# The second expert pair's second layer as seven block products over F in two halves, with its output stored transposed

## The chip, the cores and the metric

The kernel runs on one core of one Trainium2 chip. The metric is the device time of one execution in microseconds (us): 1131.18 us, the median of three runs (1131.17 to 1131.72). TensorE (PE in the rows) multiplies, VectorE (DVE) and ScalarE (ACT) do the elementwise work, SyncE (SP) issues nearly all DMA transfers, GpSimd (POOL) issues four.

## The reference, cut to what matters

```python
# retention over (batch 4, heads 8, seq 768, dim 64), then two dense experts on 3072 tokens x 512
x = attn_out.transpose(0, 2, 1, 3).reshape(B * S, H * D)          # 3072 x 512
x = _moe_ref(x, **moe);    # h = x @ w_in (512x2048); g = h - tanh(h);  x = g @ w_out (2048x512)
y = _moe2_ref(x, **moe2)   # h = x @ w_in;  g = where(h > 0, h, exp(min(h, 0)) - 1);  y = g @ w_out
```

Everything is float32. F below is the inner dimension of 2048; an "expert pair" is w_in with w_out. The change is in the last line, g @ w_out of the second pair.

## The kernel before, in words

**Arithmetic.** A float32 operand is split in two fp32r parts, a high part (a copy by ScalarE) and a low part (operand minus high part, by VectorE). A product of two operands takes three matmuls, high*high, high*low and low*high, all issued in `three` (L388, the matmul is L392). A matmul has a 128x128 stationary operand and 512 moving columns.

**Stages.** First comes retention, interleaved with the first expert pair over six blocks of 512 tokens; its result goes to DRAM (`x1d`). The weights of the second pair are unpacked meanwhile and stored as split operands: `w2d` for w_in (`weight_quad`, eight "quads" j of two 128-wide slices f = j and j + 8), `w3d` for w_out (`weight_split` and `weight_store`, 16 slices f). Then the second pair runs three times, for p = 0, 1, 2, on two blocks (1024 tokens) each.

**The second pair's first layer** is already done by Strassen's scheme in Winograd's form. Tokens are halved, the 512 input features are halved, and the two slices of a quad are the halves of F. `tokens` builds seven split token operands (`xh1`/`xl1` to `xh7`/`xl7`) from r11, r12, r21, r22. Each quad takes seven products of six matmuls, in three PSUM banks x, w, z, in the order 1, 2, 6, 7, 5, 4, 3; a product of a higher number in the list may add to a bank that an earlier one filled, and `snap` (ScalarE) or `plus` (VectorE) takes the bank's value in between. A quad's weights come as one load of 1792 KB (`q`).

**The second pair's second layer** is direct. For p, the 16 slices of F of the first token half (rows 11 and 12) are multiplied into four banks `acc3a`, the stationary operand being a 128-token piece of g and the moving one a w3 slice (512 KB load each, again for `acc3b`). The second token half is held in `ys` and multiplied into `acc3b` afterwards. Each slice is 4 banks x 3 matmuls. `split_g` makes g's two parts. The `acc3a` matmuls stand between the first layer's products (`filler`, `tails`), the `acc3b` ones behind them.

**What sets the order.** All operations after the start are given to a planner (`Plan`). Its list of TensorE operations is kept as written; the other engines' operations are ordered by due times, with tile slots and quotas per group (four `g` tiles, for instance) as limits. Each engine then runs its list in order and waits on semaphores.

Of the kernel before, what the change touches and what calls it, by code (L numbers as in the profile page):

```python
# [18 lines left out]
P = 128  # L19
TB = 512  # L20
# [226 lines left out]
def retention_moe_kernel(ctx: ExitStack, tc: tile.TileContext, dims, ins, out):  # L247
# [27 lines left out]
    w2d = [dram.tile([P, 14, HW], F32R, name=f"w2d{j}") for j in range(NQ)]  # L275
    w3d = [dram.tile([P, 2, TB], F32R, name=f"w3d{f}") for f in range(NF)]
# [120 lines left out]
    with tc.manual_schedule():  # L397
# [124 lines left out]
        for i in range(4, 12):  # L522
# [20 lines left out]
            {"raw": 12, "g": 4, "qk": 2, "pt": 1, "w1r": 5, "w3r": 5, "T": 1, "wop": 4, "r3": 1,  # L543
# [9 lines left out]
        dr = {id(t): Buf("D", name="d") for t in (*x1d, *w1d, *w2d, *w3d)}  # L553
# [54 lines left out]
        def weight_quad(j, rel):  # L608

            for f in (j, j + NQ):  # L610
                weight_raw((2, f), rel, "raw2")
                weight_32((2, f), rel)
            lo_, hi_ = W32.pop((2, j)), W32.pop((2, j + NQ))
            t = Buf("A", [P, 4, HW], F32, f"wt{j}", "T")

            def T(i):
                return t.ap[:, i, :]

            q = 0.34
            op("DVE", q, lambda: sub(T(0), hi_.ap[:, 0:HW], lo_.ap[:, 0:HW]), r=[lo_, hi_], w=[(t, 0)], name="T1")  # L620
            op("DVE", q, lambda: sub(T(1), hi_.ap[:, HW:], T(0)), r=[hi_, (t, 0)], w=[(t, 1)], name="T2")
            op("DVE", q, lambda: sub(T(2), hi_.ap[:, HW:], hi_.ap[:, 0:HW]), r=[hi_], w=[(t, 2)], name="T3")
            op("DVE", q, lambda: sub(T(3), lo_.ap[:, HW:], T(1)), r=[lo_, (t, 1)], w=[(t, 3)], name="T4")
# [4 lines left out]
            op("ACT", ACT5, lambda: copy(bh.ap[:, 0:2, :], lo_.ap.rearrange("p (a n) -> p a n", a=2)), r=[lo_], w=[(bh, 0)])  # L628
            op("ACT", 0.32, lambda: copy(bh.ap[:, 2, :], hi_.ap[:, HW:]), r=[hi_], w=[(bh, 1)])
            op("ACT", 0.95, lambda: copy(th.ap, t.ap), r=[t], w=[th])  # L630
            op("DVE", DVE5, lambda: sub(bl.ap[:, 0:2, :], lo_.ap.rearrange("p (a n) -> p a n", a=2), bh.ap[:, 0:2, :].bitcast(F32)),
               r=[lo_, (bh, 0)], w=[(bl, 0)])
            op("DVE", q, lambda: sub(bl.ap[:, 2, :], hi_.ap[:, HW:], bh.ap[:, 2, :].bitcast(F32)), r=[hi_, (bh, 1)], w=[(bl, 1)])
            op("DVE", 1.14, lambda: sub(tl.ap, t.ap, th.ap.bitcast(F32)), r=[t, th], w=[tl])
            d, k = w2d[j], dbuf(w2d[j])
            for i, (b, n) in enumerate(((bh, 3), (th, 4), (bl, 3), (tl, 4))):
                at = (0, 3, 7, 10)[i]
                dma(lambda b=b, at=at, n=n: nc.sync.dma_start(out=d[:, at:at + n, :].bitcast(F32), in_=b.ap.bitcast(F32)),
                    n * 1024, r=[b], w=[(k, i)], due=60.0)
# [114 lines left out]
        def split_g(y, name, key=None, view=None, rel=0):  # L754
            g = Buf("A", [P, 2, TB], F32R, f"g{name}", "g")
            yv = (lambda: y.ap) if view is None else (lambda: y.ap[:, view, :])
            op("ACT", ACT5, lambda: copy(g.ap[:, 0, :], yv()), r=[(y, key)], w=[(g, 0)], rel=rel, name=f"ghi{name}")
# [34 lines left out]


# [28 lines left out]
        w2_from = 2 * NF  # L822
        pend = []
        acc = None
        quads = list(range(NQ))
        w3s = list(range(NF))
# [14 lines left out]
        for b, f, lo, hi in order0:  # L841
            if b == NB - 1 and f == 0:
                block5 = now_pe()
# [16 lines left out]
            if n >= w2_from and n % 6 == 1 and quads:  # L860
                weight_quad(quads.pop(0), now_pe())
            n += 1
        assert not quads and not w3s

        XH, XL = {}, {}

        def tokens(p, rel):


            R = {}
            for i in (1, 2):
                for j in (1, 2):
                    t = R[i, j] = Buf("A", [P, 2, TB], F32, f"r{i}{j}_{p}", "r")
                    for c in range(2):
                        src = x1d[2 * p + c]
                        dma(lambda t=t, i=i, j=j, c=c, src=src: nc.sync.dma_start(
                            out=t.ap[:, :, c * HW:(c + 1) * HW],
                            in_=src[:, 2 * (j - 1):2 * j, (i - 1) * HW:i * HW]),  # L880
                            2048, r=[dbuf(src)], w=[(t, c)], rel=rel, name=f"r{i}{j}_{p}")

            def split(i, t):
                h = XH[i] = Buf("A", [P, 2, TB], F32R, f"xh{i}_{p}")
                l = XL[i] = Buf("A", [P, 2, TB], F32R, f"xl{i}_{p}")
# [15 lines left out]
            split(3, a21)  # L901

        def product(i, q, xs, dst, first, last):
            h, l = xs[i]
            k = PLACE[i]

            def fn():
# [169 lines left out]
```

## Time and profile before

| | |
|---|---|
| three runs | 1131.17, 1131.18, 1131.72 us |
| the profiled execution | 1131.98 us, of which the profile's span is 1130.1 us |
| TensorE | 5889 matmuls, busy 1109.5 us (98%) |
| weight loads | 903.7 us (80%) |
| VectorE, ScalarE | 781.4 us (69%), 664.7 us (59%) |
| DMA | 239.82 MB, mean 212 GB/s |
| chain that ended last | TensorE 96%, DMA 3%, VectorE 1% |

The page's span runs from the first to the last instruction. A matmul's record (some 390 ns) is longer than the step from one matmul to the next, since records overlap; the chain cuts the overlap away, so its pieces add up to time. In the same way records on VectorE and ScalarE overlap by some 0.1 us, and the step between two starts is what one instruction costs.

### The profile page before, as it was taken

The numbers are of one execution on the slowest core, as the hardware profiler recorded it, in microseconds if no ns is written. First come the engines' busy times: TensorE is split into PE (matmuls) and PEld (weight loads), VectorE is DVE, ScalarE is ACT, GpSimd is POOL, SyncE is SP. The second block draws the span as 40 slices with busy tenths as digits, with TensorE's granted clock in tenths as the row PEclk, the third lists the DMA queues.
The fourth block names the chain that finished last, engine by engine and source line by source line (L and its number), as shares of the span: only waits on it lengthen the run. The fifth ranks groups of instructions, "written<-read, shape, count | busy, mean of one in ns | idle before, by whom it ended". The sixth has DMA issues, their size and how long they took to land.

```text
span 1130.1 us, 15594 instructions
## 1 busy us (share of the span) xinstructions
PE 1109.5 (98%) x5889; PEld 903.7 (80%) x5889; DVE 781.4 (69%) x1274; ACT 664.7 (59%) x1194; POOL 3.8 (0%) x8
## 2 busy tenths in 40 slices
PE   7699999999999999999999999999999999999998
PEld 5588888888888888878888888888888888888887
DVE  5798899667888899788867765565465573455650
ACT  2556785455566656666756766563566662655650
POOL 0000000000000000000000000000000000000000
PEclk9799999999999999999999999999999999999999
DMA  8734375426758866677580564658455656544560
GB/s 312 279 121 164 128 252 190 129 76 225 264 195 309 297 247 255 248 281 284 218 319 1 198 233 179 237 170 352 140 205 205 237 213 267 192 176 186 209 260 38
DMA packets 67497, 239.82 MB, mean 212 GB/s; under 512 B 7264, under 2 KB 13408, under 8 KB 64352
## 3 DMA queue, kind: packets, MB, share of 16 engines
q1 hardware_dynamic: 66272, 235.96, 56.2%
q0 software_dynamic: 576, 2.10, 1.1%
q8 instruction: 46, 0.75, 0.3%
q10 hardware_dynamic: 576, 0.79, 0.2%
q14 instruction: 27, 0.22, 0.1%
HBM read 192.68 MB, written 46.14 MB: 211 GB/s over the span
## 4 chain that ended last, share of the span: by engine, by line
PE 96%; DMA 3%; DVE 1%; ACT 0%; issue 0%; SPq 0%
PE acc L392 24%; PE h L392 22%; PE x L392 12%; PE acc3a L392 12%; PE acc3b L392 12%; PE z L392 6%; PE w L392 3%; PE sc L332 2%; PE oe L362 1%; PE oe L356 1%; DMA kn<-qkv 1%; PE oo L362 1%; PE oo L370 1%; DMA stage<-qkv 1%; DMA dtab<-dtab 1%; DMA raw<-w 1%
## 5 line engine op out<-in xcount | busy, mean ns | idle before, releaser
L392 PE MATMUL acc<-g,w 128*128 128x512 f32 x1152 | 281.9, 393 | 0.0
L392 PE MATMUL h<-x,w 128*128 128x512 f32 x1152 | 278.8, 391 | 0.0
L392 PEld LDWEIGHTS h<-x,w 128*128 128x128 f32 x1152 | 217.3, 189 | 45.6 <-issue 0.2
L392 PEld LDWEIGHTS acc<-g,w 128*128 128x128 f32 x1152 | 213.3, 188 | 47.2 <-issue 0.5
L288 ACT ACTIVATE g<-y 128x512 fp32r<-128x512 f32 x144 | 90.8, 631 | 123.8 <-DVE y L731 92.5
L392 PE MATMUL acc3a<-w,g 128*128 128x512 f32 x576 | 137.1, 389 | 0.0
L392 PE MATMUL x<-xh,q 128*128 128x512 f32 x384 | 134.8, 391 | 0.0
L291 DVE TENSOR_TENSOR g<-y,g 128x512 fp32r<-128x512 f32 x144 | 99.5, 691 | 46.9 <-ACT g L288 43.5
L392 PE MATMUL acc3b<-w,gb 128*128 128x512 f32 x576 | 131.7, 389 | 0.0
L392 PEld LDWEIGHTS acc3a<-w,g 128*128 128x128 f32 x576 | 108.1, 188 | 22.7
L392 PEld LDWEIGHTS acc3b<-w,gb 128*128 128x128 f32 x576 | 108.1, 188 | 22.5
L749 DVE SCALAR_TENSOR_TENSOR y<-y,t 128x512 f32<-128x512 f32 x48 | 33.2, 692 | 124.6 <-ACT t L744 124.6
L720 ACT ACTIVATE u<-h 128x512 f32<-128x512 f32 x96 | 56.9, 593 | 79.2 <-PE h L392 79.1
L726 DVE SCALAR_TENSOR_TENSOR y<-y,u 128x512 f32<-128x512 f32 x96 | 66.1, 689 | 41.4 <-ACT y L720 41.4
L392 PEld LDWEIGHTS x<-xh,q 128*128 128x128 f32 x384 | 72.0, 188 | 17.2 <-DVE z L294 1.0
L392 PE MATMUL x<-xl,q 128*128 128x512 f32 x192 | 74.9, 390 | 0.0
L731 DVE COPY_PREDICATED y<-m,h 128x512 f32<-128x512 uint16 x96 | 70.6, 735 | 4.1 <-ACT m L720 0.9
L720 ACT ACTIVATE m<-u,xs_b 128x512 bf16<-128x512 f32 x96 | 69.5, 724 | 0.0
L720 ACT ACTIVATE y<-u,qa_b 128x512 f32<-128x512 f32 x96 | 69.3, 722 | 0.0
L392 PE MATMUL z<-xh,q 128*128 128x512 f32 x192 | 68.0, 395 | 0.0
L728 DVE SCALAR_TENSOR_TENSOR y<-y,h 128x512 f32<-128x512 f32 x96 | 65.6, 684 | 2.7 <-ACT m L720 0.5
L291 DVE TENSOR_TENSOR h<-h,t 128x512 f32<-128x512 f32 x96 | 66.5, 693 | 0.0
(92 smaller groups left out, 1317.1 us busy)
## 6 DMA issues: line engine op xcount, KB each, us to landing
w<-w3d SPq DMA_DIRECT2D x96, 512.0 KB, 8.7
q<-w2d SPq DMA_DIRECT2D x24, 1792.0 KB, 7.3
raw<-w SPq DMA_DIRECT2D x64, 512.0 KB, 7.1
w<-w1d SPq DMA_DIRECT2D x64, 512.0 KB, 6.4
qk<-qkv SPq DMA_DIRECT2D x20, 512.0 KB, 5.8
w1d<-w SPq DMA_DIRECT2D x16, 512.0 KB, 2.9
w3d<-w SPq DMA_DIRECT2D x16, 512.0 KB, 3.0
v<-qkv SPq DMA_DIRECT2D x24, 256.0 KB, 6.0
```

The lines of the kernel that those rows point to most:

```text
L288: nc.scalar.activation(out=out_, in_=in_, func=AF.Copy)
L291: nc.vector.tensor_tensor(out=out_, in0=a, in1=b, op=ALU.subtract)
L332: nc.tensor.matmul(out=sc[j][:, p, :], lhsT=qk[r, 1, p * P:(p + 1) * P], rhs=qk[r, 0, p * P:(p + 1) * P], start=True, stop=True,)
L356: nc.tensor.matmul(out=outs[p][half(p, j)], lhsT=stc[r, p, :], rhs=qk[r, 0, p * P:(p + 1) * P], start=(p < 2), stop=False, skip_group_chec ...
L362: nc.tensor.matmul(out=outs[p][half(p, j)], lhsT=v[:, h * D:(h + 1) * D], rhs=pt[:, j, p, :], start=False, stop=True, skip_group_check=True,)
L370: nc.tensor.matmul(out=ds[r, p, :], lhsT=kn[:, h * D:(h + 1) * D], rhs=v[:, h * D:(h + 1) * D], start=True, stop=True, skip_group_check=True,)
L392: nc.tensor.matmul(out=out_, lhsT=lhs(a), rhs=rhs(b), skip_group_check=True, start=(first and at == 0 and i == 0), stop=(last and at == n ...
L720: op("ACT", dur, lambda: nc.scalar.activation(out=o.ap, in_=i.ap, func=func, **kw), r=r, w=w, name=f"{func}{name}")
L726: op("DVE", DVE5, lambda: nc.vector.scalar_tensor_tensor(out=y.ap, in0=y.ap, scalar=QB, in1=u.ap, op0=ALU.add, op1=ALU.mult), r=[u], w=[y])
L728: op("DVE", DVE5, lambda: nc.vector.scalar_tensor_tensor(out=y.ap, in0=y.ap, scalar=C2, in1=h.ap, op0=ALU.mult, op1=ALU.mult), r=[h], w=[y ...
L731: op("DVE", 0.65, lambda: nc.vector.copy_predicated(out=y.ap, mask=m.ap.bitcast(U16), data=h.ap), r=[m, h], w=[y], due=9.0)
L749: op("DVE", DVE5, lambda: nc.vector.scalar_tensor_tensor(out=yv(), in0=yv(), scalar=1.0, in1=t.ap, op0=ALU.add, op1=ALU.mult), r=[t], w=[k])
```

## The change

The second layer of the second pair becomes Strassen's seven products as well. Its blocks are: the two token halves (rows), F in two halves (the inner dimension: slices j and j + 8), and the 512 output features in two halves (columns).

- `weight_quad(m, j)` now makes the seven block operands for w_out too (m = 3), and stores them in one DRAM tensor `w3d`, ordered by product. The operands' low parts stand beside the high ones, also in `w2d`. The 16 calls of it are at `quad_at` and, for the last two, in the first layer of p = 0; the 16 separate splits and stores of w_out are gone.
- The first layer keeps its products but orders them 1, 7, (3 of the quad before), 6, 2, 4, 5, and loads a quad's weights in four pieces. All four results of a quad are kept in `y` (two tiles of two).
- `second_layer` forms the sums S3, S1, S2, S4 of the activations per j on VectorE, splits seven operands of eight j each, and multiplies them in the order 1, 7, 6, 5, 4, 2, 3 into the bank pairs x, z, x, x, z, w, x. The weights are now stationary and the activations move, so the result is features by tokens; each product's weights are one 2048 KB load in one of two `X` slots. Results are stored as they stand, and the host reorders the output array at the end.
- Matmuls of the second layer: before 3 x 16 slices x 2 token halves x 4 banks x 3 = 1152; now 3 x 7 products x 8 j x 2 banks x 3 = 1008.

```diff
-    w2d = [dram.tile([P, 14, HW], F32R, name=f"w2d{j}") for j in range(NQ)]
-    w3d = [dram.tile([P, 2, TB], F32R, name=f"w3d{f}") for f in range(NF)]
+    w2d = [dram.tile([P, 7, 2, HW], F32R, name=f"w2d{j}") for j in range(NQ)]
+    w3d = dram.tile([P, 7, NQ, 2, HW], F32R, name="w3d")
...
+            for i, b in enumerate(((w1, L), b21, (w2, H))):
+                op("ACT", 0.32, lambda i=i, b=b: copy(bh.ap[:, i, :], at(b)), r=[b[0]], w=[(bh, i)])
+                op("DVE", q, lambda i=i, b=b: sub(bl.ap[:, i, :], at(b), bh.ap[:, i, :].bitcast(F32)),
+                   r=[b[0], (bh, i)], w=[(bl, i)])
...
+        quad_at = [2 * NF + 3 * NF * i // 12 for i in range(12)] + [5 * NF, 5 * NF + 3]
+        quads = [(m, j) for m in (2, 3) for j in range(NQ)]
...
-            if n >= w2_from and n % 3 == 0 and w3s:
-                for _ in range(1):
-                    f3 = w3s.pop(0)
-                    weight_raw((3, f3), now_pe(), "raw2")
-                    weight_32((3, f3))
-                    weight_split((3, f3), "wop")
-                    weight_store((3, f3), w3d[f3])
...
+            product(1, x, True)
+            s1 = snap(x, f"s1_{nm}")
+            yield
+            product(7, z, True)
+            z7 = snap(z, f"z7_{nm}")
+            yield
+            yield
+            product(6, x, False)
+            u2 = snap(x, f"u2_{nm}")
+            product(2, w, True)
+            activate(plus(w, s1, f"c11_{nm}"), 11)
+            product(4, z, False)
+            activate(plus(z, u2, f"c21_{nm}"), 21)
+            product(5, x, False)
+            activate(plus(x, z7, f"c22_{nm}", 2.0), 22)
+            yield
+            product(3, x, False)
+            activate(x, 12)
...
+        def second_layer(p, prev):
...
+            def product(i, operands, dst, first, by_e=False):
+                t = Buf("X", [P, NQ, 2, HW], F32R, f"w3_{p}_{i}")
+                k = PLACE[i]
+                dma(lambda: nc.sync.dma_start(out=t.ap.bitcast(F32), in_=w3d[:, k].bitcast(F32)),
+                    16 * 1024, r=[dbuf(w3d)], w=[t], name=f"w3_{p}_{i}")
...
+                    if (j, e) == (2, 0) and i == 1:
+                        next(prev)
...
+                        three(dst[e].ap, lambda a: t.ap[:, j, a, e * P:(e + 1) * P],
+                              lambda b: g[j].ap[:, b, :], first, True, NQ, j)
...
+            product(1, operand(11), x, True)
+            s1 = [snap(x[e], f"os1_{p}_{e}") for e in range(2)]
+            product(7, [s3(j) for j in range(NQ)], z, True)
+            z7 = [snap(z[e], f"oz7_{p}_{e}") for e in range(2)]
+            product(6, operand(11), x, False)
+            u2 = [snap(x[e], f"ou2_{p}_{e}") for e in range(2)]
+            product(5, operand(21), x, False)
+            for e in range(2):
+                store(plus(x[e], z7[e], f"oc22_{p}_{e}", 2.0), 1, 1, e)
+            product(4, operand(22), z, False)
...
+            if not last:
+                tokens(p + 1)
+            product(2, operand(12), w, True)
...
+            product(3, [s4(j) for j in range(NQ)], x, False, by_e=last)
...
-                def tail(g, f, first, last, acc_a=acc_a):
-                    weight_load(3, f, w3d[f], "w3r")
-                    second(3, W[3, f], g, acc_a, first, last)
...
-    out = nc.dram_tensor("out", (B * S, DM), F32, kind="ExternalOutput").ap()
+    out = nc.dram_tensor("out", (NCH // 2, 2, KC, P, TB), F32, kind="ExternalOutput").ap()
```

**Place 1, TensorE, first layer of p = 1, quad 1.** A tile `x1_1` is bank x of p = 1, quad 1 (its last number is only a label), `xh7_1` the high part of token operand 7. Before:

```order
L392 MATMUL z1_1_7567<-xh7_1_7205,q1_1_7360 128x512
L392 MATMUL z1_1_7567<-xl7_1_7211,q1_1_7360 128x512
L392 MATMUL z1_1_7567<-xh7_1_7205,q1_1_7360 128x512 x2
L392 MATMUL z1_1_7567<-xl7_1_7211,q1_1_7360 128x512
L392 MATMUL z1_1_7567<-xh7_1_7205,q1_1_7360 128x512
L392 MATMUL x1_1_7525<-xh5_1_7252,q1_1_7360 128x512
L392 MATMUL x1_1_7525<-xl5_1_7264,q1_1_7360 128x512
L392 MATMUL x1_1_7525<-xh5_1_7252,q1_1_7360 128x512 x2
L392 MATMUL x1_1_7525<-xl5_1_7264,q1_1_7360 128x512
L392 MATMUL x1_1_7525<-xh5_1_7252,q1_1_7360 128x512
L392 MATMUL z1_1_7567<-xh4_1_7241,q1_1_7360 128x512
L392 MATMUL z1_1_7567<-xl4_1_7254,q1_1_7360 128x512
```

Now, from the end of product 7 on:

```order
L392 MATMUL z1_1_7711<-xh7_1_7481,q1_1_1_7524 128x512
L392 MATMUL x1_0_7624<-xh3_1_7649,q1_0_3_7540 128x512
L392 MATMUL x1_0_7624<-xl3_1_7663,q1_0_3_7540 128x512
L392 MATMUL x1_0_7624<-xh3_1_7649,q1_0_3_7540 128x512 x2
L392 MATMUL x1_0_7624<-xl3_1_7663,q1_0_3_7540 128x512
L392 MATMUL x1_0_7624<-xh3_1_7649,q1_0_3_7540 128x512
L392 MATMUL x1_1_7696<-xh6_1_7597,q1_1_2_7557 128x512
L392 MATMUL x1_1_7696<-xl6_1_7610,q1_1_2_7557 128x512
L392 MATMUL x1_1_7696<-xh6_1_7597,q1_1_2_7557 128x512 x2
L392 MATMUL x1_1_7696<-xl6_1_7610,q1_1_2_7557 128x512
L392 MATMUL x1_1_7696<-xh6_1_7597,q1_1_2_7557 128x512
L392 MATMUL w1_1_7749<-xh2_1_7554,q1_1_2_7557 128x512
```

Product 4 came back to bank z after one product on another bank (5). Now three lie between (3 of quad 0, then 6 and 2, of which the last row is the start), or two at a pass's first quad. On bank x, one product lay between 1 and 6 and between 6 and 5, and now two, or one between 1 and 6 at a pass's first quad.

**Place 2, TensorE, second layer.** Before (p = 0), the second token half: banks `acc3b0_0` to `_3`, stationary a piece of the activations `gb`, moving a weight slice.

```order
L392 MATMUL acc3b0_0_7142<-w3_0_6965,gb0_0_7067 128x512 x3
L392 MATMUL acc3b0_1_7149<-w3_0_6965,gb0_0_7067 128x512 x3
L392 MATMUL acc3b0_2_7156<-w3_0_6965,gb0_0_7067 128x512 x3
L392 MATMUL acc3b0_3_7161<-w3_0_6965,gb0_0_7067 128x512 x3
L392 MATMUL acc3b0_0_7142<-w3_8_7062,gb0_8_7093 128x512 x3
L392 MATMUL acc3b0_1_7149<-w3_8_7062,gb0_8_7093 128x512 x3
L392 MATMUL acc3b0_2_7156<-w3_8_7062,gb0_8_7093 128x512 x3
L392 MATMUL acc3b0_3_7161<-w3_8_7062,gb0_8_7093 128x512 x3
```

Now (p = 1), the end of product 6 and the start of product 5 in the bank pair `xo1_0`, `xo1_1`, with the split operands `g1_6_j` and `g1_5_j`:

```order
L392 MATMUL xo1_0_8349<-g1_6_5_8577,w3_1_6_8466 128x512 x3
L392 MATMUL xo1_1_8356<-g1_6_5_8577,w3_1_6_8466 128x512 x3
L392 MATMUL xo1_0_8349<-g1_6_6_8588,w3_1_6_8466 128x512 x3
L392 MATMUL xo1_1_8356<-g1_6_6_8588,w3_1_6_8466 128x512 x3
L392 MATMUL xo1_0_8349<-g1_6_7_8598,w3_1_6_8466 128x512 x3
L392 MATMUL xo1_1_8356<-g1_6_7_8598,w3_1_6_8466 128x512 x3
L392 MATMUL xo1_0_8349<-g1_5_0_8608,w3_1_5_8555 128x512 x3
L392 MATMUL xo1_1_8356<-g1_5_0_8608,w3_1_5_8555 128x512 x3
```

Four banks per slice of F became two per j and product; products 6 and 5 follow each other on the same two banks, with `snap` to read each bank in between.

**Place 3, VectorE, second layer of p = 1.** Before, during `acc3b`: the low parts `gb1_f` of the held activations, and the next pass's token operands (`xl`, `s3`, `r21`).

```order
L291 TENSOR_TENSOR gb1_9_8462<-ys1_1_7667,gb1_9_8462 128x512
L291 TENSOR_TENSOR xl1_2_8489<-r11_2_8440,xh1_2_8477 128x1024
L291 TENSOR_TENSOR gb1_2_8484<-ys1_2_7788,gb1_2_8484 128x512
L291 TENSOR_TENSOR s3_2_8501<-r11_2_8440,r21_2_8443 128x1024
L291 TENSOR_TENSOR gb1_10_8506<-ys1_2_7788,gb1_10_8506 128x512
L291 TENSOR_TENSOR xl7_2_8520<-s3_2_8501,xh7_2_8514 128x1024
L291 TENSOR_TENSOR gb1_3_8530<-ys1_3_7909,gb1_3_8530 128x512
L294 TENSOR_TENSOR r21_2_8443<-r21_2_8443,r22_2_8448 128x1024
```

Now, during products 7 and 6: `g1_6_j` are low parts for product 6, the rows on `y1_j_0` and `y1_j_1` are the sums S2 and S1 and the last quad's activations.

```order
L291 TENSOR_TENSOR g1_6_2_8541<-y1_2_0_7875,g1_6_2_8541 128x512
L294 TENSOR_TENSOR y1_7_1_8360<-y1_7_1_8360 128x512
L291 TENSOR_TENSOR y1_5_0_8156<-y1_5_1_8186,y1_5_0_8156 128x512
L291 TENSOR_TENSOR g1_6_3_8561<-y1_3_0_7967,g1_6_3_8561 128x512
L754 SCALAR_TENSOR_TENSOR y1_7_0_8344<-y1_7_0_8344,t12_1_7_8423 128x512
L291 TENSOR_TENSOR y1_6_0_8250<-y1_6_1_8267,y1_6_0_8250 128x512
L756 TENSOR_TENSOR y1_7_0_8344<-x1_7_8255,y1_7_0_8344 128x512
L291 TENSOR_TENSOR g1_6_4_8567<-y1_4_0_8059,g1_6_4_8567 128x512
L291 TENSOR_TENSOR y1_7_0_8344<-y1_7_1_8360,y1_7_0_8344 128x512
L291 TENSOR_TENSOR g1_6_5_8577<-y1_5_0_8156,g1_6_5_8577 128x512
L291 TENSOR_TENSOR g1_6_6_8588<-y1_6_0_8250,g1_6_6_8588 128x512
L291 TENSOR_TENSOR g1_6_7_8598<-y1_7_0_8344,g1_6_7_8598 128x512
```

Before, each slice needed one row here; now an operand of product 6 needs its S1, its S2 and its low part, and the last quad's activations stand among them.

## Rows read from the trace of the kernel before

**Rows 1.** The page, its head and parts 1 and 2.

```profile
span 1130.1 us, 15594 instructions
...
PE 1109.5 (98%) x5889; PEld 903.7 (80%) x5889; DVE 781.4 (69%) x1274; ACT 664.7 (59%) x1194; POOL 3.8 (0%) x8
...
PEclk9799999999999999999999999999999999999999
```

**Rows 2.** Page part 5: line, engine, operation, count, busy us, mean ns.

```profile
L392 PE MATMUL acc3a<-w,g 128*128 128x512 f32 x576 | 137.1, 389 | 0.0
...
L392 PE MATMUL acc3b<-w,gb 128*128 128x512 f32 x576 | 131.7, 389 | 0.0
L392 PEld LDWEIGHTS acc3a<-w,g 128*128 128x128 f32 x576 | 108.1, 188 | 22.7
```

**Rows 3.** The chain that ended last, whole span: start us, us, what.

```profile
87.56 2.72 PE h L392 x12
...
754.09 38.08 PE acc3b L392 x168
...
918.40 38.08 PE acc3b L392 x168
...
1082.69 43.53 PE acc3b L392 x192
```

**Rows 4.** The same chain, asked for 628 to 754 us.

```profile
628.14 1.36 PE x L392 x6
...
662.14 1.37 PE z L392 x6
663.51 1.38 PE x L392 x6
664.89 1.43 PE z L392 x6
```

**Rows 5.** Waits of the weight-load queue, 628 to 1131 us: total, times, longest.

```profile
PEld z L392 <- ACT z L288: 3.5, 18, 0.2
```

**Rows 6.** Stretches: PE, PEld, DVE, ACT, POOL busy (x), PEclk, DMA share, GB/s.

```profile
60.00:170.00 110.00, 110.00 (x583) 90.37 (x582) 99.91 (x176) 81.28 (x149) 0.00 (x0) 1.00 0.45 168
...
766.00:772.00 6.00, 6.00 (x28) 4.99 (x27) 6.00 (x7) 2.93 (x4) 0.00 (x0) 1.00 1.01 426
```

**Rows 7.** Timeline of VectorE, 647 to 667 us: start us, us, instruction.

```profile
650.62 0.68 DVE L749 SCALAR_TENSOR_TENSOR ys<-ys,t 128x512 f32<-128x512 f32 x1
651.22 0.68 DVE L749 SCALAR_TENSOR_TENSOR y<-y,t 128x512 f32<-128x512 f32 x1
```

**Rows 8.** Timeline of ScalarE, 632 to 652 us.

```profile
633.62 0.60 ACT L288 ACTIVATE z<-z 128x512 f32<-128x512 f32 x1 [0.24 <-PE z L392]
...
649.83 0.62 ACT L744 ACTIVATE y<-u 128x512 f32<-128x512 f32 x1
650.35 0.62 ACT L744 ACTIVATE t<-u 128x512 f32<-128x512 f32 x1
```

**Rows 9.** Timeline of TensorE, 620 to 640 us.

```profile
633.19 0.39 PE L392 MATMUL z<-xh,q 128*128 128x512 f32 x1
```

**Rows 10.** Page part 6: transfers, count, KB each, median us to landing.

```profile
w<-w3d SPq DMA_DIRECT2D x96, 512.0 KB, 8.7
q<-w2d SPq DMA_DIRECT2D x24, 1792.0 KB, 7.3
```

**Rows 11.** Instructions and transfers on the tile q.

```profile
DMA to landing us min/median/max: 6.9/7.3/12.5
```

**Rows 12.** Timeline of all engines, 1116 to 1131 us.

```profile
1124.20 2.64 ACT L288 ACTIVATE o3b<-acc3b 128x512 f32<-128x512 f32 x4 [34.11 <-PE acc3b L392]
1124.83 2.37 SPq L788 DMA_DIRECT2D out<-o3b  x4
```

**Rows 13.** Groups of VectorE by form.

```profile
L291 DVE TENSOR_TENSOR wtl<-wt,wth 128x1024 fp32r<-128x1024 f32 x8 | 9.7, 1216 | 0.0
...
L291 DVE TENSOR_TENSOR wbl<-w,wbh 128x256 fp32r<-128x256 f32 x8 | 3.4, 420 | 0.0
```

More of the change, by code (lines that the diff above doesn't have):

```diff
@@ L903, in product @@
[L903 to L907, printed above, removed]
-                for c in range(2):
-                    three(dst.ap, lambda a: q.ap[:, 7 * a + k, c * P:(c + 1) * P],
-                          lambda b: (h, l)[b].ap[:, c, :], first, last, 2, c)
-            op("PE", 6 * MM, fn, r=[q, h, l], w=[dst], lat=0.2, name=f"p{i}")
+            if n == 5 * NF + 6:
+                tokens(0)
+            if n in quad_at:
+                weight_quad(*quads.pop(0), now_pe())
@@ L934, in retention_moe_kernel, with plus, bank, quad @@
-        tails = []
-        def filler(k=1):
-            for _ in range(k):
-                if tails:
-                    tails.pop(0)()
-        tokens(0, block5)
+        def plus(src, t, name, due=4.0):
+            op("DVE", DVE5, lambda: add(t.ap, src.ap, t.ap), r=[src], w=[t], due=due, name=name)
+            return t
+        def bank(name):
+            return Buf("P", [P, TB], F32, name)
+        def quad(p, j, xs):
+            nm = f"{p}_{j}"
+            q = {}
+            for ab in ((1, 7), (2, 6), (5, 4), (3,)):
+                n = len(ab)
+                t = Buf("A" if n == 2 else "B", [P, n, 2, HW], F32R, f"q{nm}_{ab[0]}", "w2r" if n == 2 else None)
+                a = PLACE[ab[0]]
+                step = PLACE[ab[-1]] - a or 1
+                dma(lambda t=t, a=a, n=n, step=step: nc.sync.dma_start(
+                    out=t.ap.bitcast(F32), in_=w2d[j][:, a:a + step * (n - 1) + 1:step].bitcast(F32)),
+                    n * 2048, r=[dbuf(w2d[j])], w=[t], name=f"quad{nm}")
+                for i, k in enumerate(ab):
+                    q[k] = t, i
+            x, w, z = bank(f"x{nm}"), bank(f"w{nm}"), bank(f"z{nm}")
+            def product(i, dst, first):
+                h, l = xs[i]
+                t, k = q[i]
+                def fn():
+                    for c in range(2):
+                        three(dst.ap, lambda a: t.ap[:, k, a, c * P:(c + 1) * P],
+                              lambda b: (h, l)[b].ap[:, c, :], first, True, 2, c)
+                op("PE", 6 * MM, fn, r=[t, h, l], w=[dst], lat=0.2, name=f"p{i}_{nm}")
+            y = Y[p, j] = {}
+            for k, pair in enumerate(((11, 12), (21, 22))):
+                t = Buf("A", [P, 2, TB], F32, f"y{nm}_{k}")
+                for i, kk in enumerate(pair):
+                    y[kk] = t, i
+            def activate(c, k):
+                t, i = y[k]
+                elu(c, f"{k}_{nm}", t, i, i)
+            product(1, x, True)
[16 more added lines that the diff above has]
+            activate(x, 12)
+            yield
@@ L942, in retention_moe_kernel @@
+        Y = {}
         for p in range(NB // 2):
             xs = {i: (XH[i], XL[i]) for i in XH}
[L944 to L986 removed]
@@ L987, in retention_moe_kernel @@
-            while tails:
-                filler()
-            evict(acc_a, out_place(p, 0), f"3a{p}")
-            if p + 1 < NB // 2:
-                tokens(p + 1, now_pe())
-            acc_b = new_acc(f"3b{p}")
-            for j in range(NQ):
-                for k in range(2):
-                    f = j + k * NQ
-                    def unit(j=j, k=k, f=f, rel=max(0, now_pe() - 10), stored=stored, acc_b=acc_b, p=p):
-                        g = split_g(stored[j], f"b{p}_{f}", k, k, rel=rel)
-                        weight_load(3, f, w3d[f], "w3r")
-                        second(3, W[3, f], g, acc_b, f == 0, f == NF - 1)
-                        if f == NF - 1:
-                            evict(acc_b, out_place(p, 1), f"3b{p}", step=1 if p == NB // 2 - 1 else 2)
-                    if p + 1 < NB // 2 and j == NQ - 1:
-                        tails.append(unit)
-                    else:
-                        unit()
+            for k, prev in enumerate(quads_in_turn(p, xs)):
+                if pend:
+                    seconds(len(pend) - 1)
+                if quads and k % 4 == 1:
+                    weight_quad(*quads.pop(0), now_pe())
@@ L1009, in retention_moe_kernel @@
+            assert not quads
+            second_layer(p, prev)
         for o, t in plan.run():
```

217 lines of the change are left out of this document (106 added, 111 removed).

## The prediction

> **What bounds the kernel now.** I read the page's head first: TensorE is busy 98% of the span at a granted clock of nine tenths or more in every slice but the start [rows 1]. Busy time overstates a matmul, so I went on to the chain of waits, whose pieces add up to time: 168 matmuls in a row take 38.08 us [rows 3], so one step is 0.2267 us, where its record is 389 ns [rows 2]. Twelve take 2.72 us in the first expert pair too [rows 3]. Then I looked for stretches where TensorE is not at that step. From the end of the start at 60 us its row shows no idle time, even where VectorE is at 99.91 of 110 us [rows 6]. The second pair is not quite full: from 754.09 to 918.40 us [rows 3] stand 720 matmuls (336 of the first layer, 384 of the second), 163.20 us by the step, in 164.31 us. The rest, 1.11 us, is in small pieces: products of six take 1.38 and 1.43 us beside 1.36 [rows 4], because bank z is wanted again before ScalarE has read it, 18 times in the weight-load queue's waits [rows 5]. So the kernel is a row of matmuls, and a matmul less is worth a step as long as operands, weights and banks come in time.
>
> **The sum, part by part.** Durations are of the profiled execution, 1131.98 us (span 1130.1); the median of the runs is 0.80 below it.
>
> 1. Matmuls. 1152 of the second layer become 1008; the first layer's 1008 stay. 144 x 0.2267 = 32.64 us, all on the path, since TensorE is the chain.
>
> A page of the Trainium skill would size this otherwise. "Perfetto Trace Analysis", section "Identifying the Most-Contended Engine", takes the busy time of weight loads as TensorE's measure; by it 144 loads of 188 ns [rows 2] would be worth 27.1 us. Here the step in an undisturbed stretch is 0.2267 us, so I keep 32.64.
>
> 2. The first layer's order. Bank z gets three other products between 7 and 4 where it had one, bank x two where it had one. The small stalls go: 1.11 us in the second pass, 1.09 in the third (918.40 to 1082.69, 164.29 us), and in the first 628.14 [rows 4] to 754.09, 125.95 us for 552 matmuls, 125.12 by the step, 0.83. Sum 3.0 us; between 0 (another wait takes their place) and 3.0, and I take all of it, since every gap but one per pass at least doubles.
>
> 3. Products 6 and 5 of the second layer follow each other on one bank pair. From the start of the last matmul on a bank to its next use are four steps, 0.91 us. A snap of a full bank stands in the rows: last matmul on z starts at 633.19 [rows 9], ScalarE reads from 633.62 for 0.60 us [rows 8], so 1.03 us at least, 0.12 late. From above: in the stalled case of [rows 4] z was 7 steps away and still 0.07 late, 1.66 us, which would be 0.75 late. Near the lower end ScalarE is free, since there is little but splits to do; I take 0.3, three times, 0.9 us (0.4 to 2.3). Behind it the whole of product 5 is queued.
>
> 4. VectorE. Its rows in products 1, 7 and 6 are the tight place. From the last read of the last quad's bank x to the low part of product 6's last operand stand 48 rows; back to back they step by 0.60 us [rows 7], 29 us, while TensorE has 12 + 6 + 36 + 48 + 48 = 150 matmuls, 34.0 us, and needs that operand six matmuls before their end, 32.6. Going through the rows with the four `g` tiles, each free only when TensorE has used it, and ScalarE's copies at 0.52 us [rows 8], I find the operand always earlier than wanted, by 1.5 to 2.5 us in product 7 and least, 0.4 us, at the fifth operand of product 6 (the last row but four of place 3), where the last quad's activations stand in front. The same count over products 2 and 3, where the next pass's seven token operands come in, gives at least 0.5. So I take 0.5 us in all; at worst, with each row at its record of 0.69 [rows 7], 43 rows up to that place are 3.9 us longer, 3.5 late a pass, 10.5 us.
>
> 5. Weights of w_out. 16 plain splits become eight quads. Of VectorE's work each quad loses two low parts of 0.69 and adds four sums and three low parts of 256 columns, 0.42 each, and a large low part of 1.22 [rows 13]: 2.8 us more, 22 us in all, and each w_in quad 0.15 (three small low parts for one of 0.69 and a small one), together 23 us; ScalarE, with one copy per low part, gets less. The cover is the first pair's matmul stream: per 16 steps of it there were 2.7 quads and 5.3 splits, and are 4 quads, about the same load, for longer, up into the first pass. TensorE waited for nothing with VectorE at 91% [rows 6], so nothing; if the cover were gone, 23 us.
>
> 6. Weight loads of the second layer, 2048 KB each. Product i's slot is free when product i - 2 is done, so the load has one product, 48 x 0.2267 = 10.88 us, to land, five times a pass; the first two of a pass have free slots. The nearest row is `q` with 1792 KB, 7.3 us in the median [rows 10, 11], by size 8.3: 2.5 us to spare. The slice loads of 512 KB (8.7 us, [rows 10]) wait in a queue of their own kind. The crowded place is product 4: the load for product 2, two stores, six token loads and a piece of the next quad, 4.7 MB, are issued ahead of the load for product 3. At the 426 GB/s that the queues moved [rows 6], 4.7 + 2.1 MB take 16.0 us of the 21.76 in two products. So nothing.
>
> The Trainium skill's "DMA: Bandwidth & Descriptors", section "Specifications", gives a lower limit from DRAM, some 358 GB/s per core. By it those 6.8 MB take 19.0 us, an estimate, the spare time halves to 2.8 us, and C below would be likelier by some 0.05. The 426 GB/s of [rows 6] lies above the limit, so C stays as it is.
>
> 7. End. The last bank is read and stored by the same steps as now, ScalarE then SP [rows 12]; four reads in 2.64 us become one, but the last of the four ends 0.6 us behind the last matmul in both. Nothing, at best 0.5 us less.
>
> Sum: 1131.98 - 32.64 - 3.0 + 0.9 + 0.5 = 1097.7 us in the profiled execution's terms, 1097.0 in the median's. Own range: 1095.0 (no new stall, shorter end) to 1101 (old stalls stay, 0.75 at each bank reuse).
>
> **Rivals.**
>
> A. VectorE becomes the bound in products 7 and 6. For it: 48 rows in 32.6 us leave it 10% and it waits for ScalarE and for `g` tiles in turn, with a smallest lead of 0.4 us in a strict order. Against: the step of 0.60 is measured back to back, and the stretch from 60 to 170 us ran with VectorE at 91% and no wait of TensorE [rows 6]. By item 4's bound 10.5 us: 1107.
>
> B. Slower than before: the weight loads of item 6 come late at each product's start. Its price is 15 loads x the lateness; it cancels the 34 us from 2.3 us late on, that is from 13.2 us for a load. For it: the slowest `q` took 12.5 us [rows 11], 14.3 by size, 3.4 late: 15 x 3.4 = 51, 1148 us. Against: that one stood behind a queue of other loads; in products 7, 6 and 5 nothing else is loaded.
>
> C. Some loads late only: the two in the crowded place and a few more, 2 to 5 us each with stores and token loads ahead, up to 20 us: 1103 to 1117. For and against as in B.
>
> **How the numbers follow.** Forecast 0.80, A 0.11, C 0.06, B 0.03. Predicted is the forecast's 1097.0. The range goes from its low end to 1104, which takes in the smaller half of A and the beginning of C and leaves out below two in ten. This kernel's runs lie within 0.05% of each other, and 0.2% (2.3 us) is about what can be told from no change. All but B are faster by more: 0.96; B is slower, 0.03; 0.01 for a mixture that ends where it began.
>
> **What would show it.** Right: `acc3a` and `acc3b` gone, 4320 matmuls of this kind in place of 4464, products of the second layer at 10.88 us each in the chain, all of 1.36 us in the first layer, and a pass (672 matmuls) at 152.3 us plus some 0.5. Item 3: a wait of product 5's first matmuls on ScalarE, three or six times. A: TensorE waits for a `g` low part on VectorE in product 7 or 6, in all three passes alike. B and C: TensorE waits on a DMA into `w` at the start of a product. Item 5: the first 628 us of the chain longer than now. The prediction is wrong if a pass takes more than 154 us, or if the first pair's end moves.

## The result, and the profile after

| | before | after |
|---|---|---|
| median of the runs on one chip | 1131.45 us (1131.17 to 1132.22, four runs) | 1100.88 us (1100.19 to 1101.49, four runs) |
| the profiled execution, its span | 1131.98 us, 1130.1 us | 1101.44 us, 1099.6 us |
| first expert pair, up to the first matmul of the second | 628.14 us [rows 4] | 632.38 us |
| second pair's matmuls, to the end of the last | 498.08 us [rows 3, 4] | 463.45 us |

The ratio is 0.9729, 95% interval 0.9712 to 0.9745. The forecast was 1097.0 us, range 1095.0 to 1104.0. The second pair gave 34.6 us, which is what the first three items of the sum ask for (32.64 + 3.0 - 0.9 = 34.7). The first pair, which the forecast left where it was, took back 4.2.

The head of the page after is to be set against [rows 1], and its last line against [rows 10]:

```profile
span 1099.6 us, 15843 instructions
...
PE 1075.6 (98%) x5745; PEld 877.7 (80%) x5745; DVE 905.5 (82%) x1516; ACT 709.6 (65%) x1290; POOL 3.9 (0%) x8
...
w<-w3d SPq DMA_DIRECT2D x21, 2048.0 KB, 8.1
```

144 matmuls are gone, VectorE has 124 us more to do, and the new loads of 2 MB take 8.1 us in the median (8.3 were estimated from `q`).

The chain of the kernel after, whole span (start us, us, what), is to be set against [rows 3]:

```profile
735.74 10.88 PE xo L392 x48
746.62 11.22 PE xo L392 x48
...
899.29 11.22 PE xo L392 x48
...
1051.96 11.22 PE xo L392 x48
...
1084.94 10.89 PE xo L392 x48
```

A product of 48 matmuls is 10.88 us, 48 steps of 0.2267, except product 5 in each pass, which is 0.34 longer. The second pass, from 790.48 to 943.15 us, is 152.67: 672 steps, 152.33, and that 0.34. Nothing else in the second pair is off the step, so what is missing lies before 632 us.

TensorE's waits in the kernel after, from 100 us on (the first line is of the matmuls, the others of the weight-load queue; total us, times, longest). Before, the same question from 100 to 640 us has no line for the matmuls:

```profile
PE sc L332 <- DMA qk<-qkv: 3.0, 3, 1.2
...
PEld acc L392 <- DVE g L291: 1.0, 2, 0.6
PEld xo L392 <- ACT ou L288: 1.9, 6, 0.4
```

The last is product 5's (six waits, two banks in three passes). The first two are in the first pair. To see where the time goes, I put the starts of the same first-layer products side by side. Before, chain in three stretches:

```profile
402.78 2.72 PE h L392 x12
...
453.59 2.72 PE h L392 x12
...
590.06 2.72 PE h L392 x12
...
600.94 2.72 PE h L392 x12
```

and after:

```profile
404.09 2.72 PE h L392 x12
...
457.09 2.72 PE h L392 x12
...
593.56 2.73 PE h L392 x12
...
605.18 2.72 PE h L392 x12
```

The delay is 1.31 us at the first, 3.50 at the second and third, 4.24 at the last. By the first matmul of every first-layer step (96 of them, counted from 0), the kernel after is 0.3 us late from the start (runs differ by that much there anyway, see the end). From step 4 on the two traces run in parallel but for five jumps: 1.01 at step 58, 0.95 at 62, 1.24 at 66, and 0.31 and 0.43 at 90 and 91. So 3.2 us belong to the waits for `qk` and 0.74 to those for `g`.

The chain of the kernel after, asked for 380 to 412 us, shows one `qk` wait from its root:

```profile
391.13 1.24 DVE wtl L291
...
392.38 0.36 SPq L642
...
392.84 7.11 DMA qk<-qkv
...
399.99 1.16 PE sc L332 x16
```

and SP's timeline there shows the queue:

```profile
391.12 0.37 SPq L642 DMA_DIRECT2D w2d<-wth  x1
392.38 0.36 SPq L642 DMA_DIRECT2D w2d<-wtl  x1
392.84 0.52 SPq L379 DMA_DIRECT2D qk<-qkv  x1
```

The load of `qk` needs nothing that VectorE makes. It stands behind the quad's last store, and that store waits for `wtl`. SP runs its list in order, so the load is issued when VectorE is done, and TensorE meets it 7.1 us later. Before, the same load was issued at 381.66 us and landed 8.9 us before its use. The cause of the meeting is in `quad_at`: twelve quads now start every four steps, and retention loads are issued every four steps too, so all of the last eleven loads stand one row behind a quad's store. Eight of them land 0.4 to 3.3 us ahead of use, three do not. The place in the list alone is not the harm: before, five of the same eleven stood right behind a quad's store too. But all eleven were issued 10.2 to 17.9 us ahead of their use, and now it is 6.4 to 9.7.

### The profile page after: what moved, and what is told of

It reads as the page before. It is cut to its first block, busy times and chain, and to the rows that moved or that the text cites. A ratio compares the mean times of both kernels' runs of the same rounds, so it can differ in the third digit from the quotient of the medians.

```text
span 1099.6 us, 15843 instructions
## 1 busy us (share of the span) xinstructions
PE 1075.6 (98%) x5745; PEld 877.7 (80%) x5745; DVE 905.5 (82%) x1516; ACT 709.6 (65%) x1290; POOL 3.9 (0%) x8
## 4 chain that ended last, share of the span: by engine, by line
PE 82%; DMA 7%; DVE 7%; ACT 2%; issue 1%; SPq 1%; DVEq 0%
PE acc L392 19%; PE h L392 17%; PE xo L392 12%; PE x L392 12%; PE z L392 6%; PE zo L392 6%; PE wo L392 3%; PE w L392 3%; DMA kn<-qkv 3%; DMA qk<-qkv 2%; PE sc L332 2%; DMA raw<-w 1%; PE oe L362 1%; DVE pt L297 1%; DVE y L733 1%
## 5 line engine op out<-in xcount | busy, mean ns | idle before, releaser
L288 ACT ACTIVATE g<-y 128x512 fp32r<-128x512 f32 x240 | 141.4, 624 | 148.6 <-DVE y L736 122.8
L291 DVE TENSOR_TENSOR g<-y,g 128x512 fp32r<-128x512 f32 x240 | 160.0, 687 | 41.4 <-ACT g L288 40.4
L392 PE MATMUL xo<-g,w 128*128 128x512 f32 x576 | 133.5, 390 | 0.0
L392 PE MATMUL x<-xh,q 128*128 128x512 f32 x384 | 127.1, 389 | 0.0
L392 PEld LDWEIGHTS xo<-g,w 128*128 128x128 f32 x576 | 107.7, 188 | 23.9 <-ACT ou L288 1.9
L754 DVE SCALAR_TENSOR_TENSOR y<-y,t 128x512 f32<-128x512 f32 x96 | 65.6, 685 | 14.7 <-ACT t L749 14.7
L392 PE MATMUL zo<-g,w 128*128 128x512 f32 x288 | 66.3, 389 | 0.0
L392 PEld LDWEIGHTS zo<-g,w 128*128 128x128 f32 x288 | 54.1, 188 | 11.2
```

What stands on the lines that cost most here:

```text
L288: nc.scalar.activation(out=out_, in_=in_, func=AF.Copy)
L291: nc.vector.tensor_tensor(out=out_, in0=a, in1=b, op=ALU.subtract)
L392: nc.tensor.matmul(out=out_, lhsT=lhs(a), rhs=rhs(b), skip_group_check=True, start=(first and at == 0 and i == 0), stop=(last and at == n ...
L754: op("DVE", DVE5, lambda: nc.vector.scalar_tensor_tensor(out=yv(), in0=yv(), scalar=1.0, in1=t.ap, op0=ALU.add, op1=ALU.mult), r=[t], w=[k])
```

## The experiments

"The changed kernel" is the one above. Each run was timed beside the kernel before, whose median was 1131.45 us beside the changed kernel, 1132.34 beside the first four runs and 1131.9 beside the others. So a run is set against the changed kernel by how far each is below the kernel before; for the changed kernel that is 30.6 us. The interval of a ratio spans 2 to 4 us, so a difference of one or two is read from the traces.

**Quads two steps later.**

```diff
-        quad_at = [2 * NF + 3 * NF * i // 12 for i in range(12)] + [5 * NF, 5 * NF + 3]
+        quad_at = [2 * NF + 2 + 3 * NF * i // 12 for i in range(12)] + [5 * NF, 5 * NF + 3]
```

> The first twelve weight quads start two first-layer steps later (steps 34, 38, ..., 78 in place of 32, 36, ..., 76); nothing is added or left out. Theory (order in SP's queue): in the changed kernel the retention loads of qk wait in SP's queue behind a quad's last store, which waits for VectorE's wtl; three of them land late and TensorE waits 1.01, 0.95 and 1.24 us at first-layer steps 58, 62 and 66. With the quads shifted the stores stand 4 to 7 rows ahead of the loads, so these 3.2 us go: steps 58 to 80 start 0.3 us or less off those of the kernel before, and the time is about 1097.7 us against 1100.9. The 0.74 us at steps 90 and 91 (VectorE late with g, beside the token sums) stays or grows a little, since quads 12 to 14 now stand closer together (78, 80, 83). Rival (VectorE is simply too full, 23 us more of work whose place does not matter): the 3.2 us stay, perhaps at other steps, and the time is 1100 to 1102 us.

Measured 1098.62 us (1098.02 to 1098.90), ratio 0.9703 (0.9687 to 0.9719). SP's timeline now has the load a few rows behind the store (start to start 3.2 us) and not held by it:

```profile
374.84 0.36 SPq L642 DMA_DIRECT2D w2d<-wtl  x1
...
377.62 0.40 SPq L606 DMA_DIRECT2D w<-w1d  x1
378.06 0.62 SPq L379 DMA_DIRECT2D qk<-qkv  x1
```

No wait for `qk` is left, and against the kernel before, the first-layer steps 4 and 80 are shifted by the same amount (both 1.0 us earlier). The waits for `g` grew from 0.74 to 1.4 us, as expected with quads at 78, 80 and 83. The theory holds, the rival fails.

**The quads' stores on another queue.** The quads stay where they are; `nc.sync.dma_start` becomes `nc.gpsimd.dma_start` for their four stores.

> The four stores of each weight quad are issued on GpSimd's DMA queue in place of SP's; the quads stay at their steps and VectorE's and ScalarE's work at its place. Theory (order in SP's queue): a retention load has no store ahead of it that waits for VectorE, so the three waits for qk (3.2 us in all) go though VectorE does the same work at the same time: about 1097.7 us. Rival (VectorE too full): VectorE's part is unchanged, so 1100 to 1102 us. A third outcome would be a cost of GpSimd's own issue (64 stores more on it); the trace of the changed kernel has only a few issues there, so this is not bounded by it: were VectorE's operations to become longer beside them, the time would be over 1102 us.

Measured 1098.46 us (1097.88 to 1098.73), ratio 0.9700 (0.9686 to 0.9715). No wait for `qk` is left; the one for `g` stays, 0.73 us. Stretch 250 to 550 us (PE, PEld, DVE, ACT, POOL busy (x), PEclk, DMA share, GB/s) of this kernel,

```profile
250.00:550.00 300.00, 300.00 (x1835) 243.77 (x1834) 258.27 (x464) 183.86 (x344) 38.43 (x50) 1.00 0.70 244
```

of the changed kernel,

```profile
250.00:550.00 300.00, 297.00 (x1820) 241.14 (x1819) 255.54 (x461) 181.83 (x341) 1.82 (x2) 1.00 0.70 242
```

and of the kernel before:

```profile
250.00:550.00 300.00, 300.00 (x1834) 243.63 (x1833) 254.70 (x447) 186.71 (x340) 1.66 (x2) 1.00 0.71 254
```

VectorE is as busy in all three, 255 to 258 us, and only the changed kernel's TensorE loses 3.00 us. So the loss is not VectorE's load: it is who waits behind VectorE. The two runs are 33.7 and 33.9 us below the kernel before, 3.1 and 3.3 more than the changed kernel. In the traces 3.2 us of waits for `qk` went (in the first, less 0.7 of longer waits for `g`).

**Product 4 between 6 and 5 in the second layer** (the lines of products 5 and 4 exchanged).

> In the second layer product 4 stands between products 6 and 5 (1, 7, 6, 4, 5, 2, 3 in place of 1, 7, 6, 5, 4, 2, 3). Theory: in the changed kernel product 5 takes 11.22 us and every other one 10.88, because its first matmuls wait until ScalarE has read bank x after product 6; with product 4 between, each of the three passes is 0.34 us shorter, 152.33 us for 672 matmuls, and the time 1.0 us lower, 1099.9 us. The first pair's waits (3.9 us) stay. Rival (0.34 us is what a product costs that follows an eviction of any bank, or the wait moves to product 4 or 3): a pass stays 152.67 us and the time 1100.9 us.

Measured 1101.06 us (1098.67 to 1101.90), ratio 0.9720 (0.9706 to 0.9735): 31.3 us below the kernel before, 0.7 more than the changed kernel, which is too little to tell from none. The chain shows that what the edit was for did happen:

```profile
889.58 10.88 PE xo L392 x48
900.46 10.88 PE zo L392 x48
911.34 10.88 PE xo L392 x48
```

All products take 10.88 us, a pass 152.32. In this execution the waits for `qk` took 4.4 us in place of 3.2 (there is a fourth, at step 50), which hides 1.0 us of gain. The term is confirmed from the trace, not from the time.

**The first layer's old order** (1, 2, 3 of the quad before, 6, 7, 5, 4).

> The first layer's products of a quarter go back to the order before (1, 2, 6, 7, 5, 4; product 3 of the quarter before after product 2), the rest as in the changed kernel. Theory: item 2 of the prediction holds, 3.0 us come from the order: z is read by ScalarE after product 7 and product 4 writes it one product later, so the stalls of the kernel before on banks z and x (7 or 8 quarters in each of three passes) come back, a pass takes about 153.7 us in place of 152.67, and the time is about 1103.9 us. Rival (the stalls came from ScalarE and VectorE being busy with the old second layer's operands, not from the order): a pass stays within 0.2 us of 152.67 and the time is 1100.9 us.

Measured 1103.44 us (1102.34 to 1104.59), ratio 0.9745 (0.9730 to 0.9760). The time is near the theory's 1103.9, but it is 28.9 us below the kernel before, so some 1.7 are lost and not 3.0, and not by the theory's cause. No wait on z or x is there. The first pass is 0.07 us longer and the third 0.10; the second is 1.28 longer, nearly all of it at the start of product 3, whose weights come late:

```profile
PE xo L392 <- DMA w<-w3d: 0.9, 1, 0.9
```

So the order did not bring the stalls back. The new copies had another edit on them that I had not priced, a due time of 2 us, by which the planner may put a copy ahead of activations. Two runs ask for it.

**No due time for the first layer's copies** (`s1`, `z7`, `u2` made with `due=None`), new order:

> The first layer keeps the changed kernel's product order, but its three copies of a bank by ScalarE (s1, z7, u2) lose their due time of 2 us and are ordered like the activations, as in the kernel before. The run with the old order and this due time showed no stalls on z and x, so the due time alone removes them. Theory 1 (order or due time, either one is enough): no stalls here, a pass 152.67 us, the time 1100.9 us. Theory 2 (the due time alone does it, the order nothing): the copies come behind activations again, products wait some 0.05 to 0.14 us each, a pass takes 153.2 to 153.8 us, the time about 1103 us.

Measured 1101.49 us (1100.97 to 1101.93), ratio 0.9732 (0.9716 to 0.9749), 30.4 us below the kernel before; passes 158.14 and 152.70 us (158.11 and 152.67 in the changed kernel). Theory 1 stands: with the new order there are no stalls without the due time either.

**Old order and no due time:**

> Old product order in the first layer and no due time for its copies of a bank: both parts of the change that bear on the banks are undone, the rest stays. If the stalls of the kernel before come from these two alone, they return: some 1.1 us a pass, a pass 153.8 us in place of 152.67, waits of TensorE's weight loads on ScalarE for z, the time about 1104 us. Rival (the stalls also needed the old second layer's operands on ScalarE and VectorE): a pass stays within 0.3 us of 152.67 and the time 1101 us.

Measured 1102.44 us (1101.34 to 1102.65), ratio 0.9740 (0.9725 to 0.9754), 29.4 us below the kernel before, so some 1.1 are lost. The second pass is 153.76 us, the number expected, and again the place is wrong (and the first and third are only 0.1 longer): products on z and x lose 0.1 us in all, and nearly all the rest is one wait at the start of product 3,

```profile
PE xo L392 <- ACT g L288: 0.7, 1, 0.7
```

which the profile puts down to ScalarE. It was the load again. In order of ScalarE's copies, the high part of that product's first operand had ended at 928.8 us, 4.3 us before the start at 933.11; the load of its weights is

```profile
L996 SPq DMA_DIRECT2D w<-w3d x1: 332/332/332, 921.6 to 921.6; - x1
...
DMA to landing us min/median/max: 11.4/11.4/11.4
```

and landed at 932.98, where the product was due at 932.24. In the run with the old order and the due times the same load took 11.6 us, in the changed kernel 10.0. So with the old order and the old due times the changed kernel still lacks the old stalls. Two runs of the kernel before, with one of the two edits each, ask what the stalls need there.

**The kernel before, with the due time:**

> The kernel before, with one edit: the first layer's copies of a bank by ScalarE (s1, u2, z7) get the due time of 2 us that the changed kernel gives them; product order and everything else stay. Theory (in the kernel before a copy stands behind ScalarE's activations and splits of other banks, so a bank is read late): the stalls of 0.83, 1.11 and 1.09 us in the three passes go or fall below 0.3 us each, a pass takes 163.3 to 163.5 us in place of 164.32, the time falls by 2 to 3 us. Rival (the order of the products sets the stalls, item 2 of the prediction as it was put): a pass stays within 0.2 us of 164.3.

Measured 1131.55 us, ratio 0.9999 (0.9990 to 1.0009), passes 164.03 and 164.24 us (164.02 and 164.32 before). The theory fails: the due time does nothing there.

**The kernel before, with the new order** (3 of the same quad last):

> The kernel before, with one edit: the first layer's products in the changed kernel's order (1, 7, 6, 2, 4, 5, then 3 of the same quarter), copies without a due time. Item 2 of the prediction as it was put (a gap of two products where there was one is enough): the stalls on z and x go, a pass 163.2 to 163.5 us in place of 164.32, the time 2 to 3 us lower. Rival (the copies come late whatever the order, by what stands ahead of them on ScalarE): a pass stays at 164 us or more.

Measured 1134.46 us (1134.34 to 1135.69), ratio 1.0027 (1.0017 to 1.0038), slightly slower. The waits on z [rows 5] are gone, and the only ones left in the second pair are three of another kind:

```profile
PE x L392 <- DVE z L294: 3.7, 3, 1.2
```

They are at each pass's last quad, where product 3 follows 5 on bank x with nothing between and waits for VectorE's sum from it, 1.53 us each. A pass is 164.74 us; without that wait 163.21, which is the step's 163.20. So in the kernel before the order alone removes the small stalls, 3.0 us, as item 2 had it, and the edit's own price of 4.6 us hides it in the time (another 1 us lies at the start and behind the last matmul).

Why the changed kernel lacks the stalls with the old order too can be read from the traces. With that order z is wanted again seven steps, 1.59 us, after the last matmul of product 7. Before, that matmul, ScalarE's copy of z and the next matmul on z are:

```profile
663.11 0.40 PE L392 MATMUL z<-xh,q 128*128 128x512 f32 x1
...
664.02 0.59 ACT L288 ACTIVATE z<-z 128x512 f32<-128x512 f32 x1
...
664.72 0.44 PE L392 MATMUL z<-xh,q 128*128 128x512 f32 x1
```

and in the run with the old order and no due time:

```profile
968.42 0.39 PE L392 MATMUL z<-xh,q 128*128 128x512 f32 x1
...
969.14 0.58 ACT L288 ACTIVATE z<-z 128x512 f32<-128x512 f32 x1
...
970.01 0.39 PE L392 MATMUL z<-xh,q 128*128 128x512 f32 x1
```

Before, the copy starts 0.91 us after that matmul in 18 of the 24 quads, the 18 waits of [rows 5]; here it starts 0.43 to 0.75 us after in 23 quads, and 0.88 in one, the only wait left on z (0.2 us in the weight-load queue). VectorE's sum on bank x likewise starts 0.98 to 0.99 us behind its matmul in 18 quads before, and 0.50 in most here. So the stalls take both, a short gap and readers that come late. The new order removes the first, and in the changed kernel the second is gone with either order. Why its readers come sooner, that is what stands ahead of them on the two engines, no run has tried.

**One more VectorE operation per j** (the line of S3 twice).

> The sum S3 of the second layer is made twice on VectorE (eight more operations of 0.60 us in each pass, all beside products 1 and 7; the result is unchanged). It measures how far rival A (VectorE bound in products 7 and 6) is away. In the changed kernel VectorE's rows from 700 to 741 us follow each other at 0.60 us without a hole, and the tightest low part, that of product 6's fifth operand, ends 1.16 us before TensorE reads it. Theory (VectorE is full there, so an extra row is late by its length): 8 x 0.60 - 1.16 = 3.6 us late, three times, 10.9 us, the time about 1111.8 us, with waits of TensorE on VectorE's g in product 6 or 7 in all three passes alike. Rival (other rows behind them give way, since VectorE's order puts what is due first): less than 1 us a pass, the time under 1104 us.

Measured 1112.56 us (1111.65 to 1114.24), ratio 0.9833 (0.9818 to 0.9847), 11.3 us less of a gain than the changed kernel, where 10.9 was expected. The first two passes take 162.18 and 156.84 us, 4.1 and 4.2 longer, where 3.6 was expected. The waits, and the chain in the first pass:

```profile
PE xo L392 <- DVE g L291: 6.9, 10, 1.3
```

```profile
744.04 0.68 DVE y L756
744.72 0.61 DVE g L291
...
745.37 5.80 PE xo L392 x23
```

The wait is in product 6, up to its fifth operand, after the last quad's activations (L756), as rival A had it. The lead there in the changed kernel can be read from VectorE's timeline,

```profile
738.80 0.69 DVE L756 TENSOR_TENSOR y<-x,y 128x512 f32<-128x512 f32 x1
739.40 0.68 DVE L291 TENSOR_TENSOR g<-y,g 128x512 fp32r<-128x512 f32 x1
```

and TensorE's

```profile
740.33 2.43 PE L392 MATMUL xo<-g,w 128*128 128x512 f32 x10
```

The low part ends at 740.08; its first reader is the fifth matmul of this row, at 740.33 + 4 x 0.2267 = 741.24: a lead of 1.16 us, the least of all operands of products 7 and 6 in each pass. By that, two extra operations a pass (1.2 us) would use it up, an estimate.

**All together:** quads at steps 26, 30, ..., 78 and product 4 between 6 and 5.

```diff
-        quad_at = [2 * NF + 3 * NF * i // 12 for i in range(12)] + [5 * NF, 5 * NF + 3]
+        quad_at = [2 * NF - 6 + 4 * i for i in range(14)]
...
```

> The fourteen quads of the first pair at steps 26, 30, ..., 78 (two more of them early, none at 80 and 83), and product 4 between 6 and 5 in the second layer. By the theory three things go: the waits for qk (3.2 us, stores 4 to 7 rows ahead of the loads), the waits for g at steps 90 and 91 (0.74 us, since no quad lies beside the token sums any more), and product 5's wait (1.0 us): 1100.9 - 4.9 = 1096.0 us. Rival (quads at 26 and 30 delay the conversion of the first expert's weights or the stores of w1, and a wait comes there): the qk and product 5 parts go and 0.5 to 3 us come back before step 34, 1097 to 1099 us.

Measured 1096.79 us (1096.39 to 1097.86), ratio 0.9693 (0.9679 to 0.9708), 35.1 us below the kernel before, 4.5 more than the changed kernel, where 4.9 was expected. From 100 us on no matmul waits on anything that the profile names. The chain, in two stretches:

```profile
628.35 1.36 PE x L392 x6
...
1079.86 10.89 PE xo L392 x48
```

The first pair ends 0.2 us from where it did before [rows 4], and the second pair's matmuls take 462.40 us, 2040 steps of 0.2267 to within 0.1. So in the second pair nothing is left but the step, and the two quads put early cost nothing that the trace shows.

## Why the prediction came out as it did

The time was inside the range and 3.9 us above the forecast; that the second pair is bound by its count of matmuls was right. But the prediction had also named a sign of being wrong, "if the first pair's end moves", and it moved by 4.24 us, by a cause that stood nowhere in it. That the time stayed in the range is in part luck: the room above 1097 was there for old stalls, dearer bank reuse, VectorE in products 7 and 6 and late weight loads, and none of these used it. By its items:

1. Right. 32.64 us; with items 2 and 3 34.7 were forecast and 34.63 came. The Trainium skill's "Perfetto Trace Analysis", section "Identifying the Most-Contended Engine", judges how near TensorE is to its limit by the share of peak FLOP/s and by the weight loads' busy share; to price matmuls by the second alone was the prediction's own step, and gave 27.1 us. The trace does not agree with that price: the weight loads' busy time fell by 26.0 us (903.7 to 877.7), the time in the second pair by the step's.
2. Right in size. The stalls are gone (3.0 us, of which 1.7 on bank x, 1.1 on z and the rest on `acc3a`), and in the kernel before the new order alone does that. It is not the whole cause: in the changed kernel ScalarE and VectorE also come to the banks sooner, and there the old order has no such stalls either.
3. Right: 0.9 forecast, 3 x 0.34 = 1.0 measured.
4. Right in place, too dark in size: nothing lost (0.5 forecast). The least lead was at product 6's fifth operand, as counted, and was 1.16 us, not 0.4. Eight more operations beside products 1 and 7 cost 4.1 to 4.2 us a pass.
5. **This failed.** "The cover is the first pair's matmul stream", the step said, and, since TensorE had waited for nothing with VectorE at 91%, "so nothing". It cost 3.9 us: 3.2 for `qk` and 0.74 for `g`. VectorE's load was the wrong thing to look at. It hardly rose between 250 and 550 us (254.70 to 255.54 us busy); the cost came from SP, whose list I had not followed there. The quads that were moved issue their stores in SP's list, at the cadence of the retention loads and just ahead of them, and a store that waits for VectorE held the loads. The `g` waits are load of the ordinary kind: from 550 us on the token sums and two quads lie beside the products, and the run without those quads there has 0.1 us of them.
6. Nothing lost, as forecast, but nearer the edge than worked out. I put 16.0 of 21.76 us for the crowded place. Product 3's load in the second pass is, after, one of

```profile
L996 SPq DMA_DIRECT2D w<-w3d x1: 332/332/332, 921.4 to 921.4; - x1
...
DMA to landing us min/median/max: 10.0/10.0/10.0
```

   it lands at 931.4 and is first read at 932.1, 0.7 us to spare and not 5.8. Two things were off. The sum let the queues run at 426 GB/s from product 4's start on; up to this load's issue they moved 307. And it had nothing behind the load: two stores, two token loads and three pieces of the next quads are issued after it and before it lands, from 921.85 us on, and share the queues, so at the 410 GB/s of the stretch

```profile
921.42:931.43 10.01, 10.01 (x46) 8.27 (x44) 10.01 (x16) 8.54 (x13) 0.00 (x0) 1.00 1.04 410
```

   4.1 MB moved, of which the load is 2.1. (By the limit in the Trainium skill's "DMA: Bandwidth & Descriptors", section "Specifications", the estimate was 2.8 us to spare. That is nearer to what came, but the trace does not agree with it as the reason, since 410 is above that limit.) Rival C was this close, and did come once in each of the two runs with the old order of the changed kernel (0.9 and 0.7 us).
7. Right: from the last matmul's end to the span's end 3.8 us after (1095.83 to 1099.6) and 3.9 before.

In one line, by the profiled executions: -32.64 - 3.0 + 1.0 + 0 + 3.9 + 0.3 (start) - 0.1 (end) = -30.5, and 1131.98 - 1101.44 = 30.5. The text had named the sign to look for, "the first 628 us of the chain longer than now", and that is where it was.

## What to carry to other kernels

When work is moved, follow its DMA issues through the issuing queue, not only its compute through the busy shares: a store that waits for a late producer delays every load behind it in an in-order list, and two periodic streams with the same period keep their distance (here all of the last eleven loads stood right behind a store). Shifting one of them by half a period, or giving the waiting stores a queue of their own, cost nothing here and showed at once whether it was the queue or the load. And a run whose time fits a theory proves little until the trace shows the wait in the place that the theory names; twice here a time (a run's, then a pass's) was near the expected one and the place was not. The engine that a profile names for a wait has to be looked up too: where its work had ended microseconds before, something else ended the wait, here a load.

## What the runs showed of the hardware

- The first 58 us differ between executions of the same instructions: against the profile of before, step 4 started from 1.0 us earlier to 0.7 later in the eleven other kernels here, whose start is the same. Differences of 1 us need the trace.
- 64 more DMA issues on GpSimd raised its busy time from 3.9 to 52.6 us, 0.76 us each by the profile, and VectorE's total stayed (905.5 and 905.7 us).
- In the changed kernel a load of 2 MB took 7.2 us with nothing else issued beside it (at 735.77 us) and 10.0 us beside the token and quad loads. A load of 512 KB into `qk`, from 250 us on, took 5.6 to 7.3 us there, and 7.4 to 10.8 in the run with all edits together, where it goes out earlier.
